# Gated attention and a long convolution: the transform split by even and odd frequencies, and score blocks turned by DMA for three chunks ahead instead of two

## The chip, the core and the metric

The kernel runs on one core of a Trainium2 chip. Five engines work side by side, each through its own instructions in order: TensorE (PE; its weight loads are listed apart as PEld), VectorE (DVE), ScalarE (ACT), GpSimd (POOL) and SyncE (SP). SP issues most DMAs and the DMA transposes, POOL issues those that load and cast the inputs, and all of them run on 16 DMA engines. The metric is the device time of one execution in microseconds, lower is better.

## The reference: what is computed

There are 8 batches of 3136 positions; u and v have 256 channels and z has 64.

```python
scores = scale * np.matmul(z, z.transpose(0, 2, 1))      # scale = 1 / 3136
attn = np.maximum(scores, 0.0) ** 2
x = u * np.matmul(attn, v)
proj = x @ w_proj                                        # 256 -> 768: x1, x2, x3
X2 = np.fft.rfft(x2, n=S, axis=1)
H = np.fft.rfft(filter_fft, n=S, axis=0)[None, :, :]
x2_conv = np.fft.irfft(X2 * H, n=S, axis=1)
out = (x1 * x2_conv * x3) @ w_out
```

The scores are symmetric, since both factors are z. The convolution over 3136 = 64 x 49 positions is a Fourier transform along the sequence, a product with the filter's spectrum, and the transform back.

## The kernel before

**Attention.** The 3136 positions stand in 25 tiles of 128 (the last is half). The columns of the score matrix are cut into 7 chunks of 512, 384, 512, 384, 512, 384 and 448 (CHUNKS). For each batch and chunk the kernel goes through the 25 tiles, two at a time; such a pair is a unit. A score matmul (line 1299) has a contraction of 64, and the two of a unit use the two halves of TensorE's rows. ScalarE applies the relu from PSUM (line 1474, to R_t), ScalarE or VectorE squares it to bf16 (lines 1481 and 1483, to A_t), and TensorE multiplies it with v (line 1329), 256 channels as two halves dh. Two units make a group; the scores of a group are one step on TensorE.

**Turned blocks.** Because the scores are symmetric, a block (tile of chunk a, columns of chunk c) is the transpose of a block that chunk a would need later. With REACH = 2, chunk c sends its blocks for chunks c+1 and c+2 through a DMA transpose from A_t to an M tile (line 1414, issued by SP), and those chunks multiply M with v without scores, relu or square. A chunk's list of units (entries) has its own and unsent tiles, the turned ones, and last the ones that it sends. The M tiles have one buffer for c+1 and two more, taken by odd and even chunks, for c+2 (m_pool).

**After a chunk.** VectorE multiplies the sum with u, which was transposed by DMA (line 1527, to xT_t). TensorE projects it: x1 and x3 (lines 847 and 859), whose product is the gate (line 865), and x2 (line 893). A first transform over 64 points with table T1 (line 724) follows for two tiles at a time, and the result goes to DRAM (spec).

**The transform.** When a batch's 7 chunks are done, add_spectrum loads the first transform's rows in another order (line 754) in 8 steps of 4 groups of frequencies, with 98 rows each: 49 frequencies as real and imaginary rows. The forward table S2 gives one matmul of 256 columns per group (line 943). VectorE forms the complex product with H in four instructions of 98 x 1024: a shuffle that swaps real and imaginary rows (line 964), two multiplies (line 967) and a difference (line 970). The inverse table TZ follows (line 1001), the result goes to DRAM, and add_end loads it back (line 765), ends the inverse transform (line 1063), multiplies by the gate (line 1070), projects (line 1101) and stores (line 1128). In the last batch the product has two multiplies (line 974) and the inverse has two matmuls per group (line 1008). The filter goes through the same transform once, in batch 0 (line 807, evicted to H). The loads of spectra and of the end share a pool of 4 buffers (spec_in).

**What sets the order.** The program is unrolled, and a planner (class Plan) writes out the order of every engine beforehand from costs of its own: TensorE takes scores (S), value matmuls (W), and the steps of projection and transform (FA, FB, FZ) in between. On the chip each engine follows that order strictly. A DMA on SP's queue starts when the ones before it have been issued.

**The start.** POOL's queue opens with the loads of v and u for batch 0 (lines 443 to 446 of the code: load_rows and cast_u), then come the index rows (iota, lines 447 to 454) that VectorE turns into the tables, T1 first (lines 612 to 621; sin_steps holds lines 588 to 596), then 8 pieces of S2 (line 644). The tables for the filter are copies of S2 (lines 792 to 794). T1 is transposed on TensorE (line 629) ahead of the first scores.

Of the kernel before, what the change touches and what calls it, by code (L numbers as in the profile page):

```python
# [11 lines left out]
P = 128  # L12
# [6 lines left out]
N1 = 64  # L19
N2 = 49  # L20
NQ = 32
KR = 2 * N2
# [7 lines left out]
REACH = 2  # L30
# [211 lines left out]
def kernel(  # L242
# [20 lines left out]
    VG = 4 * D + 16  # L263
    VW = (NT - 1) // 4 * VG + D
# [6 lines left out]
    D1 = [dram.tile([S, D], BF16, name=f"spec1_{i}") for i in range(2)]  # L271
    D2 = [dram.tile([NT * P, D], BF16, name=f"spec2_{i}") for i in range(2)]
    DF = dram.tile([S, D], BF16, name="specf")
# [26 lines left out]
    M_p = [Pool("M1", 1, [P, 1536], BF16), Pool("M2e", 1, [P, 2048], BF16), Pool("M2o", 1, [P, 1152], BF16)]  # L300
    xT_p = Pool("xT", 2, [P, 2, 512], BF16)
# [20 lines left out]
    gs_p = Pool("gs", 2, [P, 4, D], BF16)  # L322
    l_p = Pool("spec_in", 4, [P, 4, D], BF16)
# [46 lines left out]
    def halves(lo, hi):  # L370
        return [(j, lo, min(hi, NT - j)) for j in range(2) if lo < NT - j]

    def cast_z(t, b, t0, t1):
        if t1 == NT:
            nc.gpsimd.dma_start(out=t[N1:P, t1 - 1 - t0, :], in_=rows_n1(z[b])[:, NT - 1, :])
        for j, lo, hi in halves(t0, t1):
            nc.gpsimd.dma_start(
                out=t[ds(j * N1, N1), lo - t0 : hi - t0, :], in_=rows_n1(z[b])[:, NT * j + lo : NT * j + hi, :]
            )

    def cast_u(b, c):
        u_nat[b, c] = t = un_p.tile()
        t0, t1 = C0[c] // P, -(-(C0[c] + CHUNKS[c]) // P)
        if t1 == NT:
            nc.gpsimd.memset(t[N1:P, t1 - 1 - t0, :], 0.0)
        for j, lo, hi in halves(t0, t1):
            nc.gpsimd.dma_start(  # L387
                out=t[ds(j * N1, N1), lo - t0 : hi - t0, :], in_=rows_n1(u[b])[:, NT * j + lo : NT * j + hi, :]
            )
# [4 lines left out]
    def load_rows(t, src, t0=0, t1=NT):  # L394
        r = rows_n1(src)
        g0, g1 = t0 // 4, t1 // 4
        for j in range(2):
            a = NT * j
            nc.gpsimd.dma_start(
                out=t[ds(j * N1, N1), ds(g0 * VG, (g1 - g0) * VG)].rearrange("p (g x) -> p g x", x=VG)[:, :, 0 : 4 * D],  # L400
                in_=r[:, a + 4 * g0 : a + 4 * g1, :].rearrange("p (g t) d -> p g (t d)", t=4),
            )
        if t1 == NT:
            for j in range(2):
                nc.gpsimd.dma_start(out=t[ds(j * N1, N1), ds(g1 * VG, D)], in_=r[:, NT - 1, :])

    def row(t, i, n=1):
        assert i % 4 + n <= 4
        return t[:, ds(i // 4 * VG + i % 4 * D, n * D)]
# [5 lines left out]
    kcol, identf, q00 = spare[0][:, 0 : 8 * N2], spare[1][:, 0:P], spare[1][:, P : P + KR]  # L415
# [8 lines left out]
    zero = x1_p.tile()  # L424
    zero_slot = x1_p.slots.take()
    nc.vector.memset(zero[:], 0.0)
# [3 lines left out]
    z_cuts = (0, 4, 16, NT)  # L430
    for t0, t1 in zip(z_cuts, z_cuts[1:]):
        for j, lo, hi in halves(t0, t1):
            nc.sync.dma_start(
                out=zf[t0 // 16][ds(j * N1, N1), lo % 16 : lo % 16 + hi - lo, :], in_=zr[:, NT * j + lo : NT * j + hi, :]
            )
    for d2 in D2:
        nc.sync.dma_start(out=d2[S : NT * P, :], in_=zero[0:N1, 0:D])
    x1_p.slots.freed[zero_slot] = 8.0
# [4 lines left out]
    load_rows(v16[0], v[0], 0, 8)  # L443
    u_nat = {}
    cast_u(0, 0)
    load_rows(v16[0], v[0], 8, NT)
# [40 lines left out]
    def after(task, at):  # L487
        task.ready = max(task.ready, at)
        return task

    zT = {0: zT_p.tile()}
    zT_slot = {0: zT_p.slots.take()}
    z_tasks = {0: []}
# [1124 lines left out]
```

## Time and profile before

| What | Value |
|---|---|
| Runs (3) | 1052.53 us median, 1052.33 to 1054.18 |
| Profiled execution, its span from first to last instruction | 1056.2 us; the profile gives no other time for it |
| Span less median | 3.7 us (0.35%) |
| Granted TensorE clock, mean over the span | 0.990 |
| ACT relu, line 1474 | 552 instructions, 488.5 us |
| ACT square, line 1481, and DVE square, line 1483 | 276 and 276 instructions, 257.1 and 298.9 us |
| PE scores, line 1299 | 1088 matmuls, 155.1 us |
| PE values, line 1329 (from A, M, M2e, M2o) | 2688 matmuls |
| SP's DMA transposes into M, M2e, M2o | 112, 64 and 32 |

The page of the profile shows busy time by engine, 40 slices of the span in tenths, the DMA queues, and the chain of work that ended last. A busy engine need not be at its peak: matmuls overlap, and their spans run from the start to a modelled end, so the distance from start to start tells TensorE's pace. Lines are given as L and the line number; "out<-in" names what an instruction writes and reads; "[a <-b]" is the idle time before it and what ended it.

### The profile page before, as it was taken

Reading aid. Unit: us, or ns where it says so; the run is one execution under the profiler, and the core shown is the slowest. Engines: PE = TensorE matmul, PEld = TensorE weight load, DVE = VectorE, ACT = ScalarE, POOL = GpSimd, SP = SyncE. Lnnn points to the kernel's source line nnn. Section 1 sums busy time; section 2 is a strip of 40 time slices with the busy share of each in tenths; the row PEclk is TensorE's granted clock in tenths of the full one; section 3 lists DMA queues with packets and bytes.
Section 4 is the critical chain, followed back from the end, with each engine's and each line's share of the span. In section 5 each row is a group of like instructions: output and inputs, shape, how many; then the busy total and the mean of one; then the engine's idle time right before and its main releaser. Section 6 shows DMA issues by size and latency. Waiting matters only on the chain.

```text
span 1056.2 us, 18580 instructions
## 1 busy us (share of the span) xinstructions
PE 1002.7 (95%) x6335; PEld 511.0 (48%) x6335; DVE 841.3 (80%) x1449; ACT 930.4 (88%) x1326; POOL 175.9 (17%) x355
## 2 busy tenths in 40 slices
PE   5899999999999999999999999999999999999984
PEld 2443444445444544454455444545455444554573
DVE  7976678986889778997789958888788887889673
ACT  7897799997999989997999989989998899889772
POOL 3031301221022120212021310121112120001000
PEclk9999999999999999999999999999999999999997
DMA  9489836889698787898799767997789968786486
GB/s 180 74 165 162 153 76 148 151 158 178 163 162 164 136 177 168 189 154 126 169 204 180 135 139 147 181 202 130 148 163 198 179 129 158 158 187 123 115 247 202
DMA packets 325263, 168.35 MB, mean 159 GB/s; under 512 B 232766, under 2 KB 295230, under 8 KB 325168
## 3 DMA queue, kind: packets, MB, share of 16 engines
q1 hardware_dynamic: 301824, 136.19, 59.8%
q0 software_dynamic: 23344, 30.97, 20.9%
q8 instruction: 50, 0.82, 0.3%
q14 instruction: 45, 0.37, 0.1%
HBM read 90.26 MB, written 53.05 MB: 136 GB/s over the span
## 4 chain that ended last, share of the span: by engine, by line
PE 72%; DVE 9%; DMA 8%; ACT 6%; issue 3%; SPq 1%; POOL 1%; DVEq 0%; ACTq 0%; POOLq 0%
PE ps_o_t L1329 37%; PE ps_s_t L1299 11%; DMA M_t<-A_t 5%; PE ps_m_t L893 3%; PE ps_m_t L859 3%; PE ps_m_t L1101 3%; PE ps_m_t L847 3%; ACT R_t L1474 3%; PE ps_m_t L724 2%; PE ps_m_t L1001 2%; PE ps_m_t L1063 2%; DVE xT_t L1527 2%; PE ps_m_t L943 2%; DVE xh L967 1%; DMA specf<-s_t 1%
## 5 line engine op out<-in xcount | busy, mean ns | idle before, releaser
L1474 ACT ACTIVATE R_t<-ps_s_t 128x1024 f32<-128x1024 f32 (+2 forms) x552 | 488.5, 922 | 34.5 <-PE ps_s_t L1299 26.2
L1329 PE MATMUL ps_o_t<-A_t,v_t 128*128 128x512 bf16 (+2 forms) x2064 | 475.1, 355 | 1.9 <-DVE A_t L1483 1.5
L1329 PEld LDWEIGHTS <-v_t 128*128 128x128 bf16 x2688 | 253.9, 98 | 215.9 <-issue 42.2
L1483 DVE TENSOR_TENSOR A_t<-R_t 128x1024 bf16<-128x1024 f32 (+3 forms) x276 | 298.9, 1090 | 32.2 <-ACT R_t L1474 21.3
L1481 ACT ACTIVATE A_t<-R_t 128x768 bf16<-128x768 f32 (+3 forms) x276 | 257.1, 949 | 10.4 <-DMA M_t<-A_t 7.3
L1299 PE MATMUL ps_s_t<-zT_t 64*128 64x512 bf16 (+2 forms) x1088 | 155.1, 357 | 4.5 <-ACT R_t L1474 4.3
L392 POOL COPY tick<-xT_t 1x1 bf16<-1x1 bf16 x54 | 26.6, 492 | 778.7 <-DVE xT_t L1527 778.7
L1527 DVE SCALAR_TENSOR_TENSOR xT_t<-ps_o_t,uT_t 128x384 bf16<-128x384 f32 (+2 forms) x128 | 69.9, 557 | 26.2 <-PE ps_o_t L1329 16.6
L354 ACT ACTIVATE x_t<-ps_m_t 128x512 bf16<-128x512 f32 (+3 forms) x139 | 73.7, 549 | 17.0 <-PE ps_m_t L847 14.0
L1070 DVE TENSOR_TENSOR yT_t<-ps_m_t,gate_t 128x128 bf16<-128x128 f32 (+4 forms) x166 | 63.1, 425 | 27.3 <-PE ps_m_t L1063 27.1
L1299 PEld LDWEIGHTS <-zT_t 64*128 64x128 bf16 x1088 | 33.1, 94 | 103.2 <-issue 102.3
L865 DVE TENSOR_TENSOR gate_t<-ps_m_t,x_t 128x512 bf16<-128x512 f32 (+2 forms) x110 | 65.6, 618 | 20.0 <-PE ps_m_t L859 16.8
L1329 PE MATMUL ps_o_t<-M_t,v_t 128*128 128x384 bf16 (+2 forms) x336 | 77.8, 345 | 3.3 <-DMA M_t<-A_t 3.3
L358 DVE CAST x_t<-ps_m_t 128x512 bf16<-128x512 f32 (+3 forms) x90 | 54.6, 621 | 22.4 <-PE ps_m_t L893 13.4
L967 DVE TENSOR_TENSOR xh<-xh,H 98x1024 bf16<-98x1024 bf16 x112 | 72.3, 684 | 0.0
L387 POOL DMA_DIRECT2D un_t<-in_u_dram x112 | 59.7, 551 | 6.9 <-issue 4.6
L847 PE MATMUL ps_m_t<-xT_t,wp 128*128 128x512 bf16 (+2 forms) x224 | 57.5, 353 | 2.5 <-DVE xT_t L1527 1.4
L893 PE MATMUL ps_m_t<-wp,xT_t 128*128 128x256 bf16 x392 | 58.2, 273 | 1.5 <-DVE gate_t L865 1.4
L859 PE MATMUL ps_m_t<-xT_t,wp 128*128 128x512 bf16 (+2 forms) x220 | 55.5, 355 | 0.4 <-DVE gate_t L865 0.2
L354 ACT ACTIVATE xh<-ps_m_t 98x512 bf16<-98x512 f32 x86 | 50.5, 614 | 3.7 <-PE ps_m_t L943 2.5
L1329 PE MATMUL ps_o_t<-M2e_t,v_t 128*128 128x512 bf16 (+1 forms) x192 | 51.7, 370 | 1.1 <-DVE xT_t L1527 1.1
L358 DVE CAST s_t<-ps_m_t 128x512 bf16<-128x512 f32 (+2 forms) x66 | 41.4, 630 | 12.6 <-PE ps_m_t L724 10.9
(168 smaller groups left out, 1026.2 us busy)
## 6 DMA issues: line engine op xcount, KB each, us to landing
out_dram<-ost_t SPq DMA_DIRECT2D x82, 256.0 KB
spec_in_t<-spec SPq DMA_DIRECT2D x64, 196.0 KB
spec<-gs_t SPq DMA_DIRECT2D x60, 196.0 KB
spec<-s_t SPq DMA_DIRECT2D x80, 128.0 KB
v_t<-in_v_dram POOLq DMA_DIRECT2D x80, 128.0 KB, 4.1
spec_in_t<-spec SPq DMA_DIRECT2D x39, 256.0 KB
un_t<-in_u_dram POOLq DMA_DIRECT2D x56, 128.0 KB, 4.9
un_t<-in_u_dram POOLq DMA_DIRECT2D x56, 96.0 KB, 4.5
```

Source lines behind the costliest of these rows:

```text
L354: nc.scalar.activation(out_, in_, AF.Copy)
L358: nc.vector.tensor_copy(out_, in_)
L847: nc.tensor.matmul(box["p"][:, :cw], wp16[:, k, ds(nb * P, P)], xt["t"][:, k, :cw], start=(k == 0), stop=(k == 1),)
L859: nc.tensor.matmul(box["p3"][:, :cw], wp16[:, k, ds((4 + nb) * P, P)], xt["t"][:, k, :cw], start=(k == 0), stop=(k == 1),)
L893: nc.tensor.matmul(box["p"][:rows, ds(k_ * D, D)], xt["t"][:, k, ds((i + k_) * P, rows)], wp16[:, k, ds(D, D)], start=(k == 0), stop=(k == 1),
L967: nc.vector.tensor_tensor(xb["z"][:KR, i], xb["z"][:KR, i], H[:KR, qq, i], ALU.mult)
L1299: nc.tensor.matmul(ps[:m, i, :cw], zt[h, ds(t * P, m)], zt[h, ds(C0[c], cw)], start=True, stop=True)
L1329: nc.tensor.matmul(o, row(v16[b], t)[:, ds(dh * P, P)], x, start=(k == 0 and i == 0), stop=(last and i == len(pair) - 1),)
L1474: nc.scalar.activation(box["R"][:rows, 0:n, :cw], live[un][:rows, 0:n, :cw], AF.Relu)
L1481: nc.scalar.activation(a, r, AF.Square)
L1483: nc.vector.tensor_tensor(a, r, r, ALU.mult)
L1527: nc.vector.scalar_tensor_tensor(x, f, inv_s2, ut, ALU.mult, ALU.mult)
```

## The change

Two things change.

**Turned blocks.** REACH becomes 3: chunk c also sends blocks to chunk c+3. Three more M buffers are added, taken in turn by the chunk's number. The units with scores per batch become fewer, the value matmuls stay the same in number.

**The transform.** The 64-point step now takes position 49 n1 + n2 together with its mirror in n2, so that T1 sums and differences stand in the two halves of a tile; the rows of tiles are picked by runs: within a chunk the first half of a tile's rows holds n2 in descending groups, the second half in ascending ones, and v, u, z and the output are loaded and stored in pieces that end at a chunk's end. In the spectrum, 16 blocks (NJ) take the place of 32 groups: a block has two residues of 50 rows each (KB) on 128 partitions, real and imaginary parts side by side in 512 columns, and one matmul of 512 columns with a table of 128 x 128. Block 0 has four tables and four matmuls of 256 columns. The product with H is two multiplies with H repeated over the two parts, and a difference and a sum of half the length; the shuffle is gone. The last batch goes the same way as the others. Loads of the spectrum use a ring of two tiles of 8 rows, whose unused partitions POOL clears at the start, and the loads of the end have a pool of two of their own. In the gate and xT steps, the two 64-column halves of each tile become an instruction each, the first one written in reverse order of tiles. The end works by chunk and not by four tiles.

The diff, cut to its core:

```diff
-NQ = 32
-KR = 2 * N2
+NJ = 16
+KB = 50
...
-REACH = 2
+REACH = 3
...
+    M3_p = [Pool(f"M3{i}", 1, [P, 1536], BF16) for i in range(3)]
...
-    gs_p = Pool("gs", 2, [P, 4, D], BF16)
-    l_p = Pool("spec_in", 4, [P, 4, D], BF16)
+    gs_p = Pool("gs", 2, [P, 8, D], BF16)
+    l_p = Ring("spec_in", 2, [P, 8, D], BF16)
+    c_p = Pool("conv_in", 2, [P, 4, D], BF16)
...
+    def runs(lo, hi):
+        got = []
+        for c in range(NC):
+            a, b = max(lo, T0[c]), min(hi, T0[c + 1])
+            if a < b:
+                got.append((0, a, b, NT - T0[c + 1] + a - T0[c]))
+        if lo < min(hi, NT - 1):
+            got.append((1, lo, min(hi, NT - 1), NT + lo))
+        return got
...
+    def load_rows(t, src, t0, t1):
         r = rows_n1(src)
-        g0, g1 = t0 // 4, t1 // 4
-        for j in range(2):
-            a = NT * j
-            nc.gpsimd.dma_start(
-                out=t[ds(j * N1, N1), ds(g0 * VG, (g1 - g0) * VG)].rearrange("p (g x) -> p g x", x=VG)[:, :, 0 : 4 * D],
-                in_=r[:, a + 4 * g0 : a + 4 * g1, :].rearrange("p (g t) d -> p g (t d)", t=4),
-            )
+        for j, lo, hi, n2 in runs(t0, t1):
+            for c in range(home[lo], home[hi - 1] + 1):
+                a, b = max(lo, T0[c]), min(hi, T0[c + 1])
+                nc.gpsimd.dma_start(
+                    out=t[ds(j * N1, N1), ds(v_at(a), (b - a) * D)],
+                    in_=r[:, n2 + a - lo : n2 + b - lo, :].rearrange("p t d -> p (t d)"),
+                )
...
+    z_cuts, ZF = (0, 4, 14, NT), 14
...
+    load_rows(v16[0], v[0], 0, 7)
...
+    load_rows(v16[0], v[0], 7, NT)
+    k1v, k2v, k0v = kcol[:, 0:N1], kcol[:, N1 : N1 + 8 * N2], kcol[:, 456:512]
+    nc.gpsimd.iota(k1v, pattern=[[N2, N1 // 2], [0, 2]], base=0, channel_multiplier=0)
...
+    def pad_zero():
+        for t in l_p.tiles:
+            for p in (N1 // 2, N1 + N1 // 2):
+                nc.gpsimd.memset(t[ds(p, N1 // 2)].rearrange("p q d -> p (q d)").bitcast(F32), 0.0)
+
+    pads = after(on("POOL", pad_zero, 4.0, lat=0.3), 14.0)
+    s2_zero = on("POOL", lambda: nc.gpsimd.memset(S2[:].rearrange("p s m -> p (s m)").bitcast(F32), 0.0), 2.0, lat=0.3)
...
+    def by_block(d, r):
+        return d[:, :].rearrange("(b r x) d -> r b x d", r=2, x=2 * NJ)[r]
...
+            for r in range(2):
+                nc.sync.dma_start(
+                    out=box["t"][ds(r * N1, KB), 0 : 2 * nj, :], in_=by_block(src, r)[:, ds(2 * j0, 2 * nj), :]
+                )
...
+    def two_tables(ps, w, x, order):
+        for c, pair in enumerate(order):
+            for k, i in enumerate(pair):
+                nc.tensor.matmul(
+                    ps[:, ds(c * D, D)], w[:, i, :], x[:, ds(k * D, D)], start=(k == 0), stop=(k == 1)
+                )
+
+    def forward(ps, x, j):
+        if j:
+            nc.tensor.matmul(ps[:, :], S2[:, 3 + j, :], x, start=True, stop=True)
+        else:
+            two_tables(ps, S2, x, ((3, 0), (1, 2)))
+
+    def inverse(ps, y, j):
+        if j:
+            nc.tensor.matmul(ps[:, :], TZ[:, 3 + j, :], y, start=True, stop=True)
+        else:
+            two_tables(ps, TZ, y, ((3, 1), (0, 2)))
...
+    for j0 in range(0, NJ, 4):
+        ld, ibox = load_spec(DF, j0, 4, puts)
...
+                    for h, w in halves(c):
+                        g, p, x = (by_half(y, h, w) for y in (gates[b, c, nb], box["p3"], box["x"]))
+                        nc.vector.tensor_tensor(g[:, ::-1] if h == 0 else g, p, x, ALU.mult)
...
-            def swap(xb=xb):
-                z = xb["z"][:].rearrange("p i q d -> p i (q d)").bitcast(F32)
-                nc.vector.stream_shuffle(z[:, 1], z[:, 0], [i ^ 1 for i in range(32)])
...
+            def mul(i, g=g, xb=xb):
+                x = xb["x"][:].rearrange("p i (j c) d -> p i j c d", c=2)
+                h = H[:, ds(2 * g, 2), i].unsqueeze(2).to_broadcast([P, 2, 2, D])
+                nc.vector.tensor_tensor(x[:, 1 - i], x[:, 0], h, ALU.mult)
+
+            def sums(xb=xb):
+                x = xb["x"][:].rearrange("p i (j c) d -> p i c j d", c=2)
+                nc.vector.tensor_tensor(x[:, 1, 0], x[:, 1, 0], x[:, 0, 1], ALU.subtract)
+                nc.vector.tensor_tensor(x[:, 1, 1], x[:, 1, 1], x[:, 0, 0], ALU.add)
+
+            cost = c_dve2(4 * D)
+            w_ = on("DVE", lambda mul=mul: mul(0), cost, evs, prio=ZP)
+            w_ = on("DVE", lambda mul=mul: mul(1), cost, [w_], prio=ZP, lat=ZL)
+            z_ = on("DVE", sums, 2 * c_dve2(2 * D), [w_], prio=ZP)
...
+                        inverse(box["p"], xb["x"][:, 1, ds(j % 2 * 2, 2), :].rearrange("p c d -> p (c d)"), j)
...
+    def add_end(b, lasts, gtasks, cs, kind="FB", src=c_p, dsts=(o_p,), late=0, behind=(), then=()):
+        for c in cs:
+            t0, nt = T0[c], len(tiles[c])
+            w = CHUNKS[c]
...
+                    for k in range(nt):
+                        lo, hi = (nt - 1 - k) * P, k * P + N1
+                        x = cb["t"][:, k, ds(dh * P, P)]
+                        o = box["p"][:, 0:512]
+                        if hi >= w:
+                            nc.tensor.matmul(o[:, ds(lo, N1)], x, T4[:, 0:N1], start=True, stop=True)
+                            continue
+                        o = bass.AP(o.tensor, o.offset + min(lo, hi), [o.ap[0], [abs(hi - lo), 2], [1, N1]])
+                        nc.tensor.matmul(o, x, T4[:, ds(N1 if lo > hi else 0, P)], start=True, stop=True)
...
+            def store(c=c, ob=ob):
                 r = rows_n1(out[b])
-                for j in range(rows // N1):
-                    a = t0 + NT * j
-                    nc.sync.dma_start(out=r[:, a : a + nt, :], in_=ob["o"][ds(j * N1, N1), 0:nt, :])
+                for j, lo, hi, n2 in runs(T0[c], T0[c + 1]):
+                    nc.sync.dma_start(out=r[:, n2 : n2 + hi - lo, :], in_=ob["o"][ds(j * N1, N1), 0 : hi - lo, :])
...
     def m_pool(c, a):
+        if a == c + 3:
+            return M3_p[c % 3]
         return M_p[0] if a == c + 1 else M_p[1 + c % 2]
...
+                        for h, n in halves(c):
+                            x, f = by_half(xt["t"][:, dh], h, n), by_half(full[b, c, dh], h, n)
+                            ut = uT[b, c][:, 0:n, dh, ds(h * N1, N1)]
+                            x = x[:, ::-1] if h == 0 else x
+                            nc.vector.scalar_tensor_tensor(x, f, inv_s2, ut, ALU.mult, ALU.mult)
```

606 lines of the change are left out of this document (251 added, 355 removed).

## The prediction

> **What bounds the kernel now.** I read the page first, parts 1, 2 and 4.
>
> ```profile
> PE 1002.7 (95%) x6335; PEld 511.0 (48%) x6335; DVE 841.3 (80%) x1449; ACT 930.4 (88%) x1326; POOL 175.9 (17%) x355
> PE   5899999999999999999999999999999999999984
> DMA  9489836889698787898799767997789968786486
> PE 72%; DVE 9%; DMA 8%; ACT 6%; issue 3%; SPq 1%; POOL 1%; DVEq 0%; ACTq 0%; POOLq 0%
> ```
>
> TensorE is busy in every slice but the first two and the last two, and holds 72% of the chain that ended last. ScalarE and the DMA engines have little room. Matmul spans overlap, so I next asked the table of windows how little TensorE really rests, and the timeline how fast it goes.
>
> ```profile
> 176.00:440.00 264.00, 261.06 (x1654) 131.16 (x1652) 215.73 (x357) 244.79 (x347) 47.34 (x95) 1.00 0.85 165
> 440.00:704.00 264.00, 259.79 (x1654) 131.46 (x1653) 216.65 (x358) 239.36 (x335) 49.89 (x95) 1.00 0.84 163
> 704.00:968.00 264.00, 259.80 (x1647) 131.13 (x1646) 221.95 (x360) 241.14 (x343) 40.73 (x81) 1.00 0.84 161
> ```
>
> Columns: window, length, busy time of PE, PEld, DVE, ACT and POOL, granted clock (1.00), DMA share, GB/s. In these 792 us PE shows 780.7 busy: 11.3 us of rest.
>
> ```profile
> 528.38 0.39 PE L1063 MATMUL ps_m_t<-T,spec_in_t 128*128 128x128 bf16 x4
> 528.60 0.59 PE L1329 MATMUL ps_o_t<-A_t,v_t 128*128 128x512 bf16 x2
> ...
> 529.56 1.04 PE L1329 MATMUL ps_o_t<-A_t,v_t 128*128 128x512 bf16 x4
> 530.43 0.60 PE L1101 MATMUL ps_m_t<-wo,yT_t 128*128 128x256 bf16 x4
> 530.96 0.50 PE L1299 MATMUL ps_s_t<-zT_t 64*128 64x384 bf16 x4
> 531.39 0.61 PE L1101 MATMUL ps_m_t<-wo,yT_t 128*128 128x256 bf16 x4
> ```
>
> From start to start: four 512-column matmuls take 0.87 us (0.217 each, 2.4 columns a nanosecond). Four scores of 384 columns take 0.43: they run two at a time, 2 x 0.160, and 0.11 more before the next line may start. The line ahead of them took 0.53, where 4 x 0.107 was due: 0.10 more on the way in. So a **group of scores costs half its columns and about 0.20 us**. Between 176 and 968 us TensorE's own work is the bound, and what the change takes from it shortens the run.
>
> **The change part by part.** Counts come from the two programs' instruction orders; durations from the rows.
>
> 1. Scores. Units (one relu each) fall from 552 to 504: at 512 columns from 240 pairs to 224, at 384 from 224 to 192, at 448 from 72 to 56, and single tiles grow by 8 x 512 and 8 x 448. That is 8192 + 12288 + 7168 - 7680 = 19968 columns, or 8.3 us at 2.4 a nanosecond. Groups fall from 276 to 252: 24 x 0.20 = 4.8. **-13.1 us**, on the bound. The 2688 value matmuls stay.
>
> 2. Transform. Forward, per batch: 32 matmuls of 256 columns become 15 of 512 and 4 of 256 (block 0 needs two tables). Among other work the old ones cost 0.11 each:
>
> ```profile
> 198.06 0.38 PE L943 MATMUL ps_m_t<-spec_in_t,S 98*98 98x256 bf16 x2
> 198.28 0.59 PE L1329 MATMUL ps_o_t<-A_t,v_t 128*128 128x512 bf16 x2
> ```
>
> So 3.52 becomes 15 x 0.217 + 4 x 0.11 = 3.70: slightly worse, +0.18. The inverse is alike; 8 forward and 7 inverse give **+2.7**. The last batch's inverse had 64 matmuls (7.0) and now takes 3.7; it lies in the tail, where waits count more, so I take half: **-1.6**. The filter's 64 matmuls (7.0) become 3.7, and its 32 evictions 16; its line shows 3.9 us of rest, of which I take 2: **-5.3**. Table transposes fall from 32 to 19: **-0.8**.
>
> 3. Head. This part goes the other way.
>
> ```profile
> 5.10 1.14 POOL L405 DMA_DIRECT2D v_t<-in_v_dram  x2
> 6.17 0.36 POOL L447 IOTA yT_t<- 128x128 int32 x1
> 6.56 0.47 DVE L612 TENSOR_SCALAR spec_in_t<-yT_t,percol 128x64 f32<-128x64 int32 x2 [2.87 <-POOL yT_t L447]
> ...
> 8.91 0.27 PE L629 MATMUL ps_m_t<-ident,T 128*128 128x128 bf16 x1 [3.52 <-DVE T L621]
> ```
>
> The index row for the first table stands in POOL's queue behind the loads of v and u: 8 issues before, 15 after, because v now comes in pieces of one chunk. Eight took from 1.51 to 6.2 us, 0.58 each; seven more are 4.1. The table's transpose is still TensorE's fifth matmul, ahead of the first scores, and VectorE's casts of z stand behind the table's steps too. Everything starts later: **+4**. Against it, the table steps on VectorE (16 x 0.38 at L644, 8 x 1.29 at L588 to L593, 8 x 0.92 of copies at L792 to L794: 23 us) shrink to about 4, in a stretch where VectorE works 36 of 44 us: **-2**. POOL's new memsets come before its wait for the first xT, which lasts longer than they do.
>
> 4. VectorE and ScalarE. Relus: 16 x 1.036 + 32 x 0.826 + 16 x 0.923, less 8 x 0.62 and 8 x 0.56, is 48 us off ScalarE. Squares take 22 off ScalarE and 32 off VectorE (1.075 and 1.219 at 1024 columns, the rest alike); 16 fewer filter evictions are 8. The gate and xT steps become halves of 64 columns, 224 instructions each instead of 112 and 128: +17 and +15 us on VectorE (0.417 by the 256-column rows; 0.35 for 192, between 0.282 at 128 and 0.417). Its yT steps merge, -12. The product with H is, for a pair of blocks, two multiplies of 1024 (0.684 each) and two sums of 512; I put these at 0.42, the 1024 row less half its streaming: 2.2 us instead of 2.79 with the shuffle, but 2.2 instead of 1.37 in the last batch, in all -26. With the tables VectorE comes to about 785 and ScalarE to 850, each a smaller share than now: **-3** of the 11.3 us of rest (bounds 0 and -11). No row has a multiply whose H is repeated over a middle dimension. Bounds: 0.684, and 1.219, the fp32 row of L1483 at the same length; I take 0.684, whose types and length are the same. At 1.219, 128 multiplies add 68 us, and VectorE is at eight tenths, as now.
>
> [...]
>
> 5. Turning by DMA. 208 M transposes become 288, and 1076 blocks of 128 x 128 become 1448. SP spends 1.39 us on each (mean of L1414 in its rows): 111 us more in a queue that issues for some 640 of 1056. The packet records have 211328 packets of 256 bytes at a mean of 25 ns, 0.2 us of all 16 engines for a block: 372 blocks are 74 us more at a DMA share of 0.84, so about 0.91. What that costs the bound no row shows. What turned blocks cost now:
>
> ```profile
> ACT A_t L1481 <- DMA M_t<-A_t: 7.3, 4, 3.8
> PE ps_o_t L1329 <- DMA M_t<-A_t: 3.3, 4, 1.4
> ```
>
> That is 10.6 us in 8 waits. The new blocks are wanted three chunks later (some 50 us) from buffers of their own, but share the queue with the blocks for the next chunk and hold A tiles. Bounds: 0, and 43 us, if each of the 32 new sets (four a batch) costs as much as such a wait, 1.33. I take the same waits by 372/1076: **+4**.
>
> [...]
>
> 6. Tail. Loads of the last spectrum go two at a time instead of four (ring of 2), with half the data each; VectorE has 7 us more to do there, spread over 20. Bounds -3 and +4; I take 0.
>
> Sum: -13.1 + 2.7 - 1.6 - 5.3 - 0.8 + 4 - 2 - 3 + 4 = **-15.1 us**. The profiled span of 1056.2 gives 1041.1; the median of the runs lies 3.7 below that span, so the forecast is **1037.5**.
>
> **Rivals.** A, the forecast (1030 to 1045): the sum, with the small terms either way. B, a larger gain: ScalarE, 92% busy in the long windows, was behind the short rests; all 11.3 us go and the turning is hidden: -15.1 - 8.3 - 4 = -27, 1025; with a tail 3 better and a head 4 better 1018. For it: the relu and square lines have the longest busy times beside TensorE. Against: only 1.4% of rest is to be had. C, **the turning becomes the bound**. Place: a chunk that sends to three others issues up to 40 blocks, 8 us of all DMA engines, while the spectrum, v, u and output keep them half busy; the next chunk's blocks, uT and spectrum loads queue behind, and TensorE's order is fixed, so it waits. For it: DMA shares of 0.93 to 1.01 already in four windows of 44 us after 176. Against: in these TensorE still works 42.2 to 43.7. Without the +4 the sum is -19; so C decides from 0.6 us per set. At 1.33 the run gets 1052.5 - 19 + 43 = 1076; at 0.9, 1062. D, the multiply falls to 1.219: VectorE is late for scattered evictions, +5, 1042; faster still. That the change does not do what it says is excluded by the counts.
>
> **How the numbers follow.** A 0.50, B 0.20, D 0.06, C 0.24, of which 0.04 ends within 0.2% (2.1 us, about what a measurement can tell from no change) and 0.20 is slower. Faster 0.76. The range of 1018 to 1062 leaves out the far end of C (0.10) and of B (0.05).
>
> **What would show it.** Step 1: 976 score matmuls, and their busy time down by a tenth from 155. 2: 512-column lines at 0.217 start to start. 3: the table's transpose on PE near 13 us instead of 8.9. 4: multiplies near 0.68. 5: waits on M tiles no more than 15 us in total, DMA share near 0.9. If PE rests over 40 us between 176 and 968, C is right; if under 5, B. The forecast is wrong if TensorE loses its place as the bound.

## The result, and the profile after

The changed kernel takes **1094.66 us** (median of 4 runs, 1089.15 to 1099.32); the kernel before took 1053.36 beside it (4 runs). The ratio is 1.0389, 95% interval 1.0340 to 1.0439: slower by 3.9%, where 1.4% faster was forecast. The profiled execution of the changed kernel took 1089.15, with a span of 1087.3 us. The page after, the lines that answer to those of before:

```profile
PE 994.0 (91%) x5917; PEld 469.8 (43%) x5917; DVE 794.5 (73%) x1457; ACT 860.6 (79%) x1221; POOL 188.8 (17%) x405
...
PE   2898899999998999989999989999999899999954
...
DMA  7499869997999889998999978999899998977457
...
PE 68%; DMA 10%; DVE 9%; ACT 5%; issue 4%; SPq 3%; POOL 1%; DVEq 0%; ACTq 0%; POOLq 0%
```

TensorE, ScalarE and VectorE work less than before (ScalarE 860.6 instead of 930.4, VectorE 794.5 instead of 841.3), and the run is longer. TensorE has slices of 8 all along where it had 9s; in the chain DMA grew from 8% to 10% and SP's queue from 1% to 3%. The windows that the prediction used, with the same columns:

```profile
176.00:440.00 264.00, 252.89 (x1514) 119.89 (x1512) 197.31 (x360) 222.81 (x314) 45.56 (x98) 0.99 0.94 172
440.00:704.00 264.00, 251.92 (x1519) 119.17 (x1520) 204.18 (x373) 219.38 (x305) 49.36 (x106) 0.99 0.95 173
704.00:968.00 264.00, 256.25 (x1542) 121.00 (x1540) 209.33 (x381) 220.87 (x311) 43.15 (x94) 0.99 0.96 173
```

TensorE rests 30.9 us of 792, not 11.3, and the DMA share is 0.95 instead of 0.84. To see where a run gains or loses, I divide each profiled run at the first and the last start of a score matmul, which the answer for that line gives. Before and after:

```profile
L1299 PE MATMUL ps_s_t<-zT_t x1088: 319/359/631, 9.1 to 990.1; 64*128 64x512 bf16 x83, 64*128 64x384 bf16 x75, 64*128 64x448 bf16 x24
```

```profile
L1284 PE MATMUL ps_s_t<-zT_t x976: 319/360/632, 19.4 to 1019.4; 64*128 64x512 bf16 x93, 64*128 64x384 bf16 x79, 64*128 64x448 bf16 x24
```

Head 9.1 to 19.4 (**+10.3 us**), steady part 981.0 to 1000.0 (**+19.0**), tail 66.2 to 67.9 (**+1.7**): together the 31.1 us by which the span grew. The line between steady part and tail is not the same work in both: after the last score 130 value matmuls were still to come before, and 93 are now, and in the tail TensorE rests 26.5 us where it rested 19.7.

**The head.** The timeline of the changed kernel's start (start us, length, then the instruction):

```profile
10.15 1.14 POOL L417 DMA_DIRECT2D v_t<-in_v_dram  x2 [1.63 <-DMA un_t<-in_u_dram]
11.68 0.52 POOL L417 DMA_DIRECT2D v_t<-in_v_dram  x1 [0.39 <-DMA v_t<-in_v_dram]
...
13.30 0.52 POOL L422 DMA_DIRECT2D v_t<-in_v_dram  x1 [0.41 <-DMA v_t<-in_v_dram]
13.82 0.32 POOL L458 IOTA yT_t<- 128x64 int32 x1
14.18 0.85 DVE L631 TENSOR_SCALAR gs_t<-yT_t,percol 128x32 f32<-128x32 int32 x4 [10.68 <-POOL yT_t L458]
...
17.04 0.95 DVE L362 CAST xT_t<-ost_t 128x256 bf16<-128x256 f32 x1
...
18.14 0.58 PE L543 MATMUL ps_m_t<-ident,xT_t 128*128 128x128 bf16 x4 [18.14 <-DVE xT_t L362]
18.52 0.31 PE L641 MATMUL ps_m_t<-ident,T 128*128 128x128 bf16 x1
```

The index row leaves POOL's queue at 13.82 (6.17 before). Ahead of it stand 17 issues, not the 15 that the prediction counted: the first ten go out by 6.83 us without a wait, 0.53 us each, and most of those behind them also wait for earlier loads to land, up to 1.63 us. VectorE stands still for 10.68 us, and its cast of z stands behind the table's steps (with the row first, in e1 below, it runs at 5.46); so TensorE's first matmul is at 18.14, not 4.78.

**The steady part.** The waits of the changed kernel that matter (who waits, for what: us in total, times, longest):

```profile
PE ps_s_t L1284 <- ACT R_t L1459: 19.1, 17, 4.1
...
DVE A_t L1468 <- DMA M_t<-A_t: 14.7, 7, 3.7
...
ACT A_t L1466 <- DMA M_t<-A_t: 11.8, 5, 3.8
DVE A_t L1468 <- DMA M2e_t<-A_t: 10.0, 3, 4.7
...
ACT A_t L1466 <- DMA M2e_t<-A_t: 7.5, 4, 2.9
```

The names M_t and M2e_t on the right are the transfers that read an A tile; M_t takes in the new M3 tiles. Squares waited 44.0 us in 19 places for an A tile that a turning transfer still read; before it was 9.1 in 5 (7.3 on ScalarE, in the prediction's lines, and 1.8 on VectorE):

```profile
DVE A_t L1483 <- DMA M_t<-A_t: 1.8, 1, 1.8
```

No value matmul waits for an M tile in the changed kernel. What stands behind the waiting square on its engine waits as well. One such place, with only the instructions concerned:

```profile
340.59 0.38 PE L794 MATMUL ps_m_t<-spec_in,S 128*128 128x512 bf16 x1
...
342.69 1.06 ACT L1466 ACTIVATE A_t<-R_t 128x1024 bf16<-128x1024 f32 x1 [3.67 <-DMA M_t<-A_t]
343.65 0.58 ACT L358 ACTIVATE xh<-ps_m_t 128x512 bf16<-128x512 f32 x1
...
344.28 0.40 PE L800 MATMUL ps_m_t<-xh,TZ 128*128 128x512 bf16 x1 [3.31 <-ACT xh L358]
344.50 2.10 PE L1314 MATMUL ps_o_t<-A_t,v_t 128*128 128x384 bf16 x6
```

A square on ScalarE waits 3.67 us; an eviction of the transform is queued behind it; TensorE rests 3.31 us for that eviction. And the rest has a second price: the next six matmuls of 384 columns take 2.10 us, where four took 0.81 and eight 1.46 shortly before. The windows over three such stretches show why, in the last column but two:

```profile
95.30:98.70 3.40, 2.95 (x8) 1.04 (x8) 1.33 (x5) 0.40 (x1) 0.18 (x1) 0.51 1.22 274
...
344.50:347.90 3.40, 3.40 (x11) 1.01 (x9) 1.90 (x4) 2.16 (x3) 0.00 (x0) 0.50 0.84 172
...
849.70:853.10 3.40, 3.40 (x11) 1.18 (x12) 2.22 (x6) 1.17 (x3) 0.00 (x0) 0.50 1.00 220
```

The granted clock is 0.50 for 3.4 us. The changed kernel has six such stretches between 25 and 960 us, about 10 us lost (6 x 3.4 x 0.5); the kernel before has one, at 116.97. The six start at 95.34, 129.47, 344.51, 378.64, 631.23 and 849.68 us, which are 10, 63, 10, 74 and 64 times 3.41 us apart. In the 3.4 us before each of the six, TensorE worked 1.6 us at most; two of these, then two over which a rest of 3.41 us (486.1 to 489.5) is split, and behind which the clock stays at 1.00:

```profile
341.10:344.50 3.40, 0.22 (x2) 0.10 (x2) 0.60 (x1) 1.81 (x3) 0.00 (x0) 1.00 0.81 195
375.20:378.60 3.40, 1.52 (x12) 0.78 (x13) 1.28 (x2) 3.04 (x4) 0.00 (x0) 1.00 0.80 220
...
484.45:487.86 3.41, 1.62 (x9) 0.69 (x7) 1.34 (x2) 0.00 (x0) 0.00 (x0) 1.00 1.04 223
487.86:491.27 3.41, 1.78 (x10) 0.61 (x10) 1.10 (x2) 2.75 (x5) 0.00 (x0) 1.00 0.32 86
```

### The profile page after: what moved, and what is told of

Read it like the earlier page. It is cut to its first block, busy times and chain, and to the rows that moved or that the text cites. A ratio compares the mean times of both kernels' runs of the same rounds, so it can differ in the third digit from the quotient of the medians.

```text
span 1087.3 us, 17763 instructions
## 1 busy us (share of the span) xinstructions
PE 994.0 (91%) x5917; PEld 469.8 (43%) x5917; DVE 794.5 (73%) x1457; ACT 860.6 (79%) x1221; POOL 188.8 (17%) x405
## 4 chain that ended last, share of the span: by engine, by line
PE 68%; DMA 10%; DVE 9%; ACT 5%; issue 4%; SPq 3%; POOL 1%; DVEq 0%; ACTq 0%; POOLq 0%
PE ps_o_t L1314 35%; PE ps_s_t L1284 9%; DMA M_t<-A_t 5%; PE ps_m_t L1087 4%; DMA M2e_t<-A_t 3%; PE ps_m_t L867 3%; PE ps_m_t L855 3%; PE ps_m_t L898 3%; ACT R_t L1459 2%; PE ps_m_t L800 2%; PE ps_m_t L794 2%; PE ps_m_t L1056 2%; PE ps_m_t L732 2%; DVE xh L970 2%; DVE A_t L1468 2%
## 5 line engine op out<-in xcount | busy, mean ns | idle before, releaser
L1459 ACT ACTIVATE R_t<-ps_s_t 128x1024 f32<-128x1024 f32 (+5 forms) x504 | 436.1, 904 | 49.2 <-PE ps_s_t L1284 25.4
L1468 DVE TENSOR_TENSOR A_t<-R_t 128x1024 bf16<-128x1024 f32 (+5 forms) x250 | 266.9, 1074 | 75.4 <-ACT R_t L1459 44.8
L1466 ACT ACTIVATE A_t<-R_t 128x768 bf16<-128x768 f32 (+4 forms) x254 | 234.6, 932 | 28.1 <-DMA M_t<-A_t 11.8
L1284 PE MATMUL ps_s_t<-zT_t 64*128 64x512 bf16 (+2 forms) x976 | 146.0, 361 | 20.1 <-ACT R_t L1459 19.1
L1314 PE MATMUL ps_o_t<-M_t,v_t 128*128 128x384 bf16 (+2 forms) x560 | 134.8, 346 | 1.6 <-DVE xT_t L1508 1.5
L875 DVE TENSOR_TENSOR gate_t<-ps_m_t,x_t 128x256 bf16<-128x256 f32 (+1 forms) x222 | 72.2, 382 | 39.7 <-PE ps_m_t L867 36.5
L1508 DVE SCALAR_TENSOR_TENSOR xT_t<-ps_o_t,uT_t 128x256 bf16<-128x256 f32 (+1 forms) x224 | 76.1, 381 | 30.4 <-PE ps_o_t L1314 20.8
L970 DVE TENSOR_TENSOR xh<-xh,H 128x1024 bf16<-128x1024 bf16 x120 | 80.8, 683 | 6.8 <-ACT xh L358 6.2
L1059 DVE TENSOR_TENSOR yT_t<-ps_m_t,gate_t 128x512 bf16<-128x512 f32 (+2 forms) x99 | 59.2, 619 | 28.2 <-PE ps_m_t L1056 26.1
L417 POOL DMA_DIRECT2D v_t<-in_v_dram x112 | 59.4, 553 | 6.9 <-issue 2.3
L855 PE MATMUL ps_m_t<-xT_t,wp 128*128 128x512 bf16 (+2 forms) x222 | 55.4, 353 | 2.9 <-DVE xT_t L1508 2.6
```

The source lines that it names most:

```text
L855: nc.tensor.matmul(box["p"][:, :cw], wp16[:, k, ds(nb * P, P)], xt["t"][:, k, :cw], start=(k == 0), stop=(k == 1),)
L970: nc.vector.tensor_tensor(x[:, 1 - i], x[:, 0], h, ALU.mult)
L1284: nc.tensor.matmul(ps[:m, i, :cw], zt[h, ds(t * P, m)], zt[h, ds(C0[c], cw)], start=True, stop=True)
L1314: nc.tensor.matmul(o, row(v16[b], t)[:, ds(dh * P, P)], x, start=(k == 0 and i == 0), stop=(last and i == len(pair) - 1),)
L1459: nc.scalar.activation(box["R"][:rows, 0:n, :cw], live[un][:rows, 0:n, :cw], AF.Relu)
L1466: nc.scalar.activation(a, r, AF.Square)
```

## The experiments

Theory 1, stated after the two profiles were compared: the third set of turned blocks costs the steady part, by its transfers. Rival: the new transform does. Beside them the head theory (the order of POOL's queue) and, within theory 1, three mechanisms: bytes on the DMA engines, A tiles held, issue in SP's queue. "Head" is the first score matmul, "steady" the time from it to the last one, both in the profiled run. That run is not always a typical one: it lay 9.6 us above its median in e6 and 5.0 in e9, and below it by 7.3 in e19, 7.5 in e4 and 5.5 in the changed kernel. The versions ran in groups, each beside the kernel before, whose median moved by 2.7 us between them; so small differences are told by the ratios too.

| Kernel | median us | ratio to before, 95% | head | steady |
|---|---|---|---|---|
| before | 1053.4 to 1056.1 | 1 | 9.1 | 981.0 |
| changed | 1094.66 | 1.0389 (1.0340-1.0439) | 19.4 | 1000.0 |
| e1_index_first | 1084.33 | 1.0304 (1.0243-1.0365) | 7.2 | 1006.1 |
| e2_reach2 | 1066.73 | 1.0154 (1.0082-1.0226) | 19.4 | 977.6 |
| e5_no_third_dma | 1064.28 | 1.0087 (1.0058-1.0116) | 20.0 | 972.5 |
| e4_a10 | 1091.03 | 1.0343 (1.0282-1.0404) | 18.7 | 986.7 |
| e6_dummy_turns | 1105.48 | 1.0514 (1.0458-1.0570) | 19.6 | 1027.8 |
| e8_half_dose | 1096.26 | 1.0402 (1.0370-1.0435) | 19.8 | 1003.4 |
| e5b_no_third_dma_a10 | 1067.18 | 1.0127 (1.0099-1.0156) | 18.9 | 971.8 |
| e9_reach2_first_l4 | 1070.81 | 1.0164 (1.0114-1.0214) | 7.2 | 1003.4 |
| e10_small_out | 1084.94 | 1.0279 (1.0223-1.0335) | 19.4 | 991.8 |
| e11_half_02 | 1062.88 | 1.0074 (1.0048-1.0100) | 19.5 | 974.0 |
| e12_small_dummy | 1157.40 | 1.0992 (1.0919-1.1065) | 19.3 | 1069.6 |
| e13_reach2_first | 1063.95 | 1.0072 (1.0033-1.0110) | 7.2 | 984.8 |
| e14_sets_012 | 1093.52 | 1.0377 (1.0327-1.0427) | 19.7 | 999.8 |
| e15_sets_023 | 1072.42 | 1.0178 (1.0138-1.0218) | 19.4 | 978.3 |
| e16_small_dummy | 1092.24 | 1.0366 (1.0321-1.0409) | 19.2 | 1007.1 |
| e17_old_transform_02 | 1105.97 | 1.0516 (1.0466-1.0566) | 9.1 | 1025.5 |
| e18_small_third | 1076.04 | 1.0184 (1.0141-1.0226) | 18.4 | 988.7 |
| e19_sets_02_first | 1053.18 | 0.9968 (0.9943-0.9994) | 7.2 | 970.4 |

**Turning or transform: e2 and e5.**

```diff
-REACH = 3
+REACH = 2
```

> The even-and-odd transform alone: blocks are turned for two chunks as before (REACH 2). Theory 1, that the third set of turned blocks costs the steady part some 23 us (13 us of saved scores lost and 10 more): about 1069, which is the kernel before with 13 of head and 8 of tail, less the transform's own 6. Theory 2, that the transform itself (halves of 64 columns, pairs of blocks, loads two at a time) slows the steady part: the saved scores come back on top, 1100 or more.

```diff
-                    mirrors[b, c, a] = m_pool(c, a).tile()
+                    mirrors[b, c, a] = M3[c % 3] if a == c + 3 else m_pool(c, a).tile()
+                if a == c + 3:
+                    return
```

> The changed kernel, instruction by instruction, but the turning transfers of the third set are left out: the value matmuls of those tiles read tiles of zeros instead, so that part of the values is missing from the sum. Scores stay at 976 matmuls. Theory 1, that the third set's transfers cost the 23 us (by their load on the DMA engines or by holding A tiles): 1068 to 1075, with head and tail still 21 us longer than before. Theory 2, that the transform slows the steady part: 1090 or more.

Both came out as theory 1 had it, a little under its figures: 1066.7 and 1064.3. The changed kernel and e5 have the same order on TensorE, VectorE, ScalarE and POOL (but for three clears on VectorE at the start of e5), so that the 80 transfers alone cost **30 us** (1094.7 less 1064.3; 27.5 of the steady part). The transform alone is 3.4 us faster in the steady part between the two profiles, but that does not hold: by the medians e2 is 11.9 us slower than the kernel before, 1.6 more than the head explains, and e13 below, whose head is shorter than that of the kernel before, is still 0.7% slower. And the saved scores, without their transfers, take only 5.1 us off the steady part (977.6 to 972.5; 2.5 by the medians, 7 by the ratios, whose intervals overlap), not 13.1. In e5 these waits are left:

```profile
PE ps_s_t L1287 <- ACT R_t L1464: 13.1, 15, 2.4
...
ACT A_t L1471 <- DMA M2e_t<-A_t: 8.4, 4, 3.2
DVE A_t L1473 <- DMA M2e_t<-A_t: 6.3, 2, 4.4
ACT A_t L1471 <- DMA M_t<-A_t: 5.0, 2, 3.0
...
DVE A_t L1473 <- DMA M_t<-A_t: 3.7, 1, 3.7
```

Scores waiting for relus are 13.1 us here and 1.8 in e2: much of what TensorE saves in scores it now rests. That ScalarE is late there because squares wait for the old transfers is a reading of these lines, and e5b below does not bear it out.

**More A tiles: e4 and e5b.**

```diff
-    A_p = Pool("A", 8, [P, 1024], BF16)
+    A_p = Pool("A", 10, [P, 1024], BF16)
```

> The changed kernel with ten A tiles instead of eight. If the price of the third set is paid because squares wait for A tiles that transfers still read (44 us of such waits in 19 of the longest places), two more tiles take 5 to 15 us off: 1080 to 1090. If the transfers as such are too many for the DMA engines, buffers only put off the wait: 1091 to 1095.

> e5_no_third_dma (the third set's transfers left out, tiles of zeros read instead) with ten A tiles instead of eight. The scores saved seem to have brought it only some 5 us in the steady part, where 13 were counted; 23 us of squares waiting for A tiles are left there. If these waits hide the rest of the saving: 1054 to 1059. If not (the scores are just worth less than counted): 1062 to 1066.

1091.0, its interval overlapping that of the changed kernel, and 1067.2, not faster than e5. Two more tiles do not pay. In e4 they do not remove the waits either: squares wait 44.0 us in 19 places, as with eight, so that this run cannot tell what the waits themselves cost. In e5b the waits fall from 23.4 to 16.1 us and nothing is gained. (The steady part in the table flatters both runs: with ten tiles 125 value matmuls come after the last score, with eight 93.)

**The head: e1, e13 and e9.** The iotas and the memset are moved ahead of load_rows in POOL's queue:

```diff
     nc.gpsimd.iota(pi_i[:], pattern=[[0, 1]], base=0, channel_multiplier=1)
+    nc.gpsimd.iota(k1v, pattern=[[N2, N1 // 2], [0, 2]], base=0, channel_multiplier=0)
+    ...
```

> The changed kernel with the index rows for the tables (three iotas, a memset) ahead of the loads of v and u in POOL's queue; all else the same. Head theory: the first matmul comes at 18.1 us instead of 4.8 because the first index row ends at 13.8 us behind fifteen loads; with the rows first, the first matmul is back at 5 to 6 us, and the whole run is 9 to 13 us shorter (1082 to 1086). Rival, that the DMA engines set the pace of the run after the head: the first matmul moves likewise, but the end by less than 5 us (1090 to 1095).

> The transform alone with the index rows first in POOL's queue, two load buffers as in the change. Against e2_reach2 (1066.7) the first matmul comes 12 us earlier. If the steady part keeps its pace: 1055 to 1058. e9_reach2_first_l4, with four load buffers besides, gave 1070.8: if that loss came from the early start (the loads of v and u later by the index rows), this run shows it too, 1065 to 1072; if from the four buffers, this run is at 1055 to 1058.

> The transform alone (two chunks turned), the index rows first in POOL's queue, and four buffers instead of two for the loads of the spectrum. Head theory: 10 us less than e2_reach2 from the earlier start. Tail: in the last batch the product waits for loads that go two at a time; four buffers take 2 to 4 us off there, or nothing if VectorE's 2.2 us for a pair of blocks sets the pace. Together 1052 to 1058, which would be level with the kernel before (1054.8).

The start of e1, with only the same steps:

```profile
1.36 0.29 POOL L440 IOTA yT_t<- 128x64 int32 x1
...
3.55 0.80 DVE L631 TENSOR_SCALAR gs_t<-yT_t,percol 128x32 f32<-128x32 int32 x4
...
5.46 0.34 DVE L362 CAST xT_t<-ost_t 128x256 bf16<-128x256 f32 x1
...
5.95 0.27 PE L543 MATMUL ps_m_t<-ident,xT_t 128*128 128x128 bf16 x1 [5.95 <-ACT T L617]
```

The first matmul is at 5.95, and e1 is 10.3 us shorter by the medians (ratio 1.0389 to 1.0304, 9 us; the intervals overlap a little). The same edit takes 9.7 us (11 by the ratios) off e11, clear of noise, in e19 below: the head theory holds. Of 12.2 us in the head, 6 are given back in the steady part of e1's profile. e13 gains less against e2, 2.8 us by the medians and 8.6 by the ratios, and at 1063.95 it lies between its two forecasts: part of what the earlier start should bring is lost later, and why stays open. e9 differs from e13 by four load buffers instead of two. It was to gain 2 to 4 us in the tail and gained 3.5 there (63.3 instead of 66.8), but the run is 6.9 us longer by the medians, 10 by the ratios. The 18.6 between the steady parts in the table overstate it, since e9's profile is its slowest run. TensorE waits 5.1 us for M tiles in four places there; that earlier loads of the spectrum collide with the turning fits this, and isn't shown.

**Bytes, issue, or tiles held: e6, e10, e12, e16, e18.** e6 turns the third set though nobody reads it (the condition in mirror becomes `c < a <= c + 3`, with REACH = 2):

> The transform with blocks turned for two chunks (as e2_reach2), but the blocks for the third chunk are turned as well, and nobody reads them: 288 turning transfers as in the changed kernel, 1088 score matmuls as in the kernel before. Theory 1, that the load itself (and the A tiles that it holds) is the price: e2_reach2's 1066.7 and about 27 us more, 1088 to 1098. Rival, that the price comes from the fixed order of the values that read the third set, or from the shorter chunks with fewer scores: 1067 to 1075, since nothing waits for these blocks.

1105.5, 39 us above e2 and above both forecasts: nobody waits for these blocks, so the price is not in the values that read them. e10 cuts the stores of the output to 4 of 64 rows in six batches:

> The changed kernel in its own order, with the stores of the output cut to 4 of 64 rows in the first six batches (most of the output is not written; every store is still issued): about as many bytes less on the DMA engines as the third set added. If the price of some 30 us comes from the total load on the DMA engines, it goes wherever the bytes are saved: 1063 to 1072. If it belongs to the turning transfers (their queue, their latency, the A tiles they hold), it stays: 1085 to 1094.

1084.9, at the lower edge of the second; 9.7 us of the price went. The total load on the DMA engines is not the price: all packets together took 874 us of the 16 engines instead of 974, no more than in e5 (868), and the run is 21 us longer than e5. But by the packet records the saved bytes lie mostly in chunks 0 to 2 of a batch, and in chunk 4 the packets still fill 1.06 of the 16 engines' time, as in the changed kernel (chunks divided at their first score, mean of the six middle batches). So bytes at the wrong moment may still be to blame. e12 makes each unread transfer one block, and had a fault:

> e6_dummy_turns in its own order (all engines issue the same), but each of the 80 unread transfers turns one block of 128 columns instead of three to eight. If what costs in e6_dummy_turns (1105.5) is the blocks moved and the time for which they hold A tiles: 1067 to 1075, near e2_reach2. If it is the issue of 80 more transfers in SP's queue (some 1.4 us each), or the order that the planner makes around them: 1095 to 1105.

```profile
SPq L1400 <- DMA M_t<-A_t: 89.6, 25, 7.0
```

1157.4. Each small transfer wrote where the last one had, and SP waited 89.6 us for its own landings. That is no answer to the question. e16 gives each transfer columns of its own:

> e12_small_dummy without its fault: there, each small transfer wrote the same columns as the one before, and SP waited 90 us for its own landings. Here each writes columns of its own; the order of all engines is that of e6_dummy_turns (1105.5), with one block per unread transfer instead of three to eight. If bytes on the DMA engines are the price: 1067 to 1078. If the count of transfers in SP's queue, or the order planned around them: 1095 to 1106.

1092.2: of 39 us, 13 go with the bytes and 25 stay. Against e12, whose other instructions are the same, it prices SP's queue: without the 89.6 us in which SP stood still the run is 65 us shorter. Since the planner's order in e6 and e16 differs from e2's as well, e18 does the same within the changed kernel's own order:

```diff
+                if a == c + 3:
+                    nc.sync.dma_start_transpose(out=m[:, ds(j * P, rows)], in_=live[un][:rows, ds(i * cw, P)])
+                    return
                 nc.sync.dma_start_transpose(out=o, in_=live[un][:rows, ds(i * cw, len(ts) * cw)])
```

> The changed kernel in its own order, with every transfer of the third set issued as before, but each turning only one block of 128 columns instead of three to eight; the rest of those tiles is read as zeros, so that part of the values is missing. Between e5_no_third_dma (none of them, 1064.3) and the changed kernel (1094.7). If the bytes are the price: 1066 to 1074. If the issue in SP's queue and the A tiles held until a transfer lands, however small it is: 1085 to 1095. In e6 and e16 a third of the price were bytes and two thirds the rest; by that 1080 to 1086.

1076.0, between the first range and the forecast from e6 and e16: with one block each, 80 transfers cost **12 us** over e5; the other **19 us** come with the rest of the blocks. The order is kept here, so this split is the better one; how much of the 12 is issue on SP and how much A tiles held is not separated.

**Which set: e8, e11, e14, e15.** A tuple THIRD names the chunks that send to c+3:

```diff
+    def reach(c):
+        return 3 if c in THIRD else 2
```

> The changed kernel with the third set turned from two of the four chunks only (the 384-column ones, chunks 1 and 3): 256 turning transfers, half the extra blocks, half the saved scores. If the price grows evenly with the blocks, it lies half way between e2_reach2 (1066.7) and the changed kernel (1094.7): 1078 to 1083. If it is a matter of a full DMA that begins at some load, it is nearer to one end: 1064 to 1072 if the threshold is not reached.

> The other half of the third set: turned from the 512-column chunks 0 and 2 only. The half from chunks 1 and 3 cost as much as the whole (1096). If any extra turning brings the whole price: 1090 to 1097 again. If the price sits with the sets of chunks 1 and 3: 1064 to 1070.

> The changed kernel with the third set turned from chunks 0, 1 and 2, without the one from chunk 3 to chunk 6. The sets from 0 and 2 cost nothing (1062.9), those from 1 and 3 the whole 30 us. If the price is the burst at the end of chunk 3 (it would send to 4, 5 and 6: nearly every A tile of that chunk is held by a transfer, and the DMA engines stand at 1.01 in the chunk behind it): 1058 to 1066. If it is the set from chunk 1 to chunk 4: 1085 to 1097.

> The counterpart: the third set from chunks 0, 2 and 3, without that from 1 to 4. If the burst of chunk 3 is the price: 1085 to 1097. If the set from 1 to 4: 1058 to 1066. If neither alone reaches it, and only the sum of the load over chunks 2 to 4 does: both runs at 1063 to 1080.

Chunks 1 and 3: 1096.3, the whole price and outside both ranges. 0 and 2: 1062.9, 3.9 us below e2 with intervals that touch, so these two sets are hidden at least; that they pay is shown by e19 against e13 below. 0, 1, 2: 1093.5. 0, 2, 3: 1072.4. So the set from chunk 1 to chunk 4 costs some 30 us on top of 0 and 2, that from 3 to 6 some 10, and not one on top of the other. The burst of chunk 3 is not the main price. The squares' waits for A tiles are longer where the price is: 9.7 us in e11, 21.5 in e15, 34.7 in e8, 47.3 in e14. The load of chunk 4 does not go with it: the packets' share there is 1.07 in e14 and 1.06 in the changed kernel, but 1.05 in e15 and 1.01 in e2, which pays nothing, and in e8 it is 0.88 at the whole price. Each of these versions has an order planned anew, and an order that suits it badly is a rival that was not tried. Why this one set is so dear stays open.

**The good half: e17 and e19.**

> The kernel before, with its own transform, and the third set turned from chunks 0 and 2 alone (23 gate tiles instead of 26, to make room). On the new transform these two sets took 4 us off while they added 37 us of 16 engines. If they are free here as well: 1046 to 1052, faster than the kernel before (1054). If the old transform, whose loads are spread otherwise, leaves less room for them: 1055 to 1070.

1106.0, some 50 us slower than the kernel before and far outside both ranges. The sets and the gate tiles (23 instead of 26) were changed together, and which of them, or the loads of the old transform, is the reason wasn't tried. It does not look like the price of the changed kernel over again: TensorE rests 50 of the 792 us from 176 to 968 at a DMA share of 0.83, and squares wait only 18.6 us for A tiles. e19 is e11 with the index rows first:

> The best pieces together: the transform, the third set from chunks 0 and 2 alone, and the index rows first in POOL's queue. e11_half_02 had 1062.9 with the first score matmul at 19.5 us; with it at 7.2 and the steady part as it was: 1050 to 1054, level with the kernel before or a little faster. If the earlier start is given back in the steady part, as in e13_reach2_first (9 of 12 us lost): 1057 to 1062.

```profile
176.00:440.00 264.00, 258.64 (x1577) 122.52 (x1574) 215.47 (x386) 233.30 (x330) 49.35 (x106) 1.00 0.91 172
440.00:704.00 264.00, 259.75 (x1579) 122.59 (x1578) 213.32 (x385) 234.08 (x324) 49.38 (x106) 1.00 0.92 174
704.00:968.00 264.00, 262.01 (x1619) 125.67 (x1617) 213.44 (x380) 229.35 (x320) 38.26 (x85) 1.00 0.82 169
```

1053.18 against 1056.11, ratio 0.9968 (0.9943 to 0.9994): level with the kernel before or **0.3% faster**, the only version that is not slower. Against e13, which differs by the two sets alone, it is 10.8 us faster (11 by the ratios), clear of noise. In its profile, which is the fastest of 12 runs (1045.9), TensorE rests 11.6 us in these windows, no more than before, at a DMA share of 0.88 and a granted clock of 1.00.

## Why the prediction was wrong, point by point

On spans, the forecast was 1041.1 and the profile has 1087.3: 46 us. (The medians differ by 11 more, because the profiled run before lay above its median and the one after below.) Of the 57 us between the medians, by the medians of e2 and e5, 26 lie in step 5, 11 in step 1, 10 in steps 2, 4 and 6 together and 8 in step 3, each a few us either way.

1. **Scores, -13.1.** The work went as counted: 976 matmuls, 146.0 us instead of 155.1. The gain did not: 2.5 to 7 us without any new transfer (e5 against e2). The step took rest as fixed while work is removed; scores waiting for relus rose from 1.8 to 13.1 us. Where the transfers have room, half of the saving (6.5 us by the count) gave 3.9 us by the medians from e2 to e11 and 10.8 from e13 to e19: the size is plausible, its condition was missing.
2. **Transform, -5.0 with the filter and the tables.** Not shown: -3.4 in the steady part of e2's profile, but +1.6 by the medians with the head taken off, and e13 is 0.7% (0.3 to 1.1) slower than the kernel before although it starts earlier. What eats the saving stays open.
3. **Head, +4 - 2.** Measured +10.3: mis-sized. There are nine more issues and not seven, and 0.58 us an issue was the rate of a queue that does not wait; behind the tenth issue POOL waits for landings as well, up to 1.63 us. And the step counted only the table's own way, though it had said that the cast of z stands behind it.
4. **Relief, -3.** None. The engines' busy time was predicted well (785 and 850; measured 794.5 and 860.6, the multiplies 0.683 where 0.684 was taken), but e5, which has all of the relief and none of the new transfers, rests 18.5 us from 176 to 968, where the kernel before rests 11.3. For the multiply, the prediction took the lower of its two bounds, and the trace agrees; the sums of 512, put at 0.42, took 0.42 to 0.43 (lines 974 and 975):

```profile
L970 DVE TENSOR_TENSOR xh<-xh,H 128x1024 bf16<-128x1024 bf16 x120 | 80.8, 683 | 6.8 <-ACT xh L358 6.2
```

5. **Turning, +4.** This is the step that failed: measured +30 (27.5 of it in the steady part), 0.94 us for each of 32 sets, above the 0.6 from which rival C decides and within its bounds (0 to 43). The count of blocks and the 74 us of DMA time were right (the packets' time rose by 76, from 327 to 403: 47616 more of them, again at 25 ns). What failed is the scaling of today's waits by 372/1076: with 35% more blocks the squares' waits for A tiles went from 9.1 to 44.0 us, while those of values for M tiles vanished. Rival C named the cause, but with the wrong place: by the waits it is not values waiting for M, and not spectrum loads, but squares waiting for A tiles, and behind them whatever stands on ScalarE and VectorE. That the transfers cost the 30 us is shown; that these waits carry all of it is not, since no run removed them alone. C's sign "PE rests over 40 us between 176 and 968" was not met: 30.9, and 6.8 more that look like work, lost in the four half-clock stretches that lie there. With 0.94 a set C's own sum gives 1064; the other 31 us are the head and the savings that did not come.
6. **Tail, 0, with -1.6 for the last inverse.** +1.7 by the division at the last score, though 37 fewer value matmuls lie behind it.

## What to carry to other kernels

A transfer that reads a buffer is a user of that buffer (here squares waited 44.0 us for A tiles that transfers still read): before adding transfers that nobody waits for, ask who needs the tile that they hold, and what is queued behind that one. With the DMA engines 0.84 busy, 76 us more of their time cost 30 and 39 us of the run (the changed kernel, e6), not the 4 that today's waits suggested; try each part of such an addition alone, since here two of four sets paid and one cost nearly all. And compare medians before believing a gain that one profile shows. When a load is cut into more pieces, look at what stands behind it in the same queue at the start: here the index row went out at 13.82 us instead of 6.17.

## What the runs showed of the hardware

In the profiled runs of the two kernels, between 25 and 960 us, TensorE's granted clock fell to 0.50 for stretches of 3.41 us: once before, six times in the changed kernel. I count both runs in steps of 3.41 us from these starts. Five steps at full clock had TensorE resting 2.0 us or more (2.47 us in the kernel before; 3.41, 3.18, 2.65 and 2.50 in the changed kernel), and a step at half clock followed each. Of three steps with 1.8 to 2.0 us of rest, two were followed by one (1.94 at 126.06 and 1.85 at 375.23) and one was not (1.94 at 436.67). Of 528 with less rest, none was, the two with 1.80 and 1.62 us that share the rest from 486.1 to 489.5 among them. From 60 to 968 us TensorE rested 16.0 us in e2, 40.1 in the changed kernel, 46.5 in e6 and 84.0 in e12; the granted clock of the windows there (60 to 176, then 264 us each) was 1.00 in e2, 0.97 to 0.99 in the changed kernel and in e6, and 0.95 to 0.97 in e12. Turning transfers of one block each, 80 of them, cost 12 us of the run where those of three to eight blocks cost 30 (e18), and 25 where those cost 39 (e16). A 128x128 tensor_scalar on VectorE took 1.09 us at 15.70 us in the changed kernel, while POOL issued loads (its clear of a tile begins at 16.65), and 0.28 in e1.
